# An attention and gated-MLP kernel: the first chunk of rows passes its first two projection blocks in two column halves, with another order of work around them

## The chip, the core and the metric

One core of one Trainium2 chip runs the kernel. Its engines take their instructions each in its own program order: TensorE (PE; its weight loads are listed apart as PEld), VectorE (DVE), ScalarE (ACT), GpSimd (POOL) and SyncE (SP), which here only starts transfers. The metric is the device time of one execution in microseconds (us), lower is better.

## The reference, cut to what matters

```python
x = A_x                                     # (1, 2048, 576), float32
xn = _layernorm(x, axis=-1)                 # (x - mean) / sqrt(var + 1e-5), per row
s = _A_ref(xn, A_wqkv, A_wo)                # attention: 32 heads of 18, then @ wo
g = _silu(_B_ref(xn, B_w_gate, B_w_up, B_w_down))   # ((xn Wg) * (xn Wu)) Wd, F = 4608
return x + s * g

def _A_ref(x, wqkv, wo):
    qkv = (x @ wqkv) ...                    # 576 -> 3 * 576
    p = softmax(q k^T * 18 ** -0.5)
    return (p v) ... @ wo
```

## The kernel before

The 2048 rows are worked in four chunks of 512, each of four tiles of 128 rows. The change lies wholly in the first tens of microseconds, in which chunk 0 is normalised, turned and multiplied with the first q and k weights. The rest of the program (attention, the gated MLP and the output projection, some 2500 us) stands in the same order before and after.

A product is made nearly float32-exact out of two float32r parts: a "high" copy, rounded on ScalarE, and a "low" rest, subtracted on another engine. So a column tile `xc` of a chunk has nine slices (four of 128 features high, the same four low, and slice 8, which holds the last 64 features high in its lower and low in its upper partitions), and one block of 128 output features is 14 matmuls, listed in `PAIRS`: nine with high weights, then five with low ones. There are nine blocks (0 to 8) for q and k.

The steps for chunk 0, with the lines of the profile:

- `load_x` (L289) loads the four row tiles into `xin`; `w_fetch` (L105, L109) loads weights into `wraw`, whose two buffers hold two blocks each, and `w_last` loads the last 64 features of a second block into `wl`. All go through SP's queue, in program order.
- `norm` takes statistics on VectorE (L298, L299) and a square root on ScalarE (L300). `norm_apply` then takes the reciprocal and the offset on VectorE (L308, L310), scales the tile on ScalarE (L311) and copies the last 64 columns beside themselves on GpSimd (L312). Chunks 2 and 3 scale on VectorE instead (L314, L316).
- `w_now` splits the weights of a buffer (`w_piece`): high on ScalarE (L451; for blocks 0 and 1 on VectorE, L449), low on GpSimd (L452).
- `to_columns` turns the tiles on TensorE (20 transposes of 128x128; L345 for chunk 0, L354 otherwise) into five PSUM banks of 512 columns, and converts each bank: high on ScalarE (L357, L361), low on VectorE (L358, L362).
- `qk_block(b, c)` multiplies block b with chunk c (L368, 14 matmuls of 512 columns) into a PSUM bank (`pa` or `pb`, two buffers each, in turn), and ends it: high on ScalarE (L371), low on VectorE (L372), both into `hl`, which SP stores to `sqk` (L378).

The program calls, for chunk 0: loads; `norm(0)`; `w_now(0)` (blocks 0, 1); `to_columns(0)`; `w_now(1)` (blocks 2, 3); `norm(1)`; the fetch of blocks 4 and 5; then blocks 0, 1, 2; `to_columns(1)`; `w_now(2)` (blocks 4, 5); blocks 3, 4, 5, with `norm(2)` and the split of the v weights (`v_split`, L414, L415) among them.

## Time and profile before

| | |
|---|---|
| median of 3 runs | 2564.52 us (2563.38 to 2564.65) |
| the profiled execution | 2566.68 us; its span from first to last instruction is 2564.9 us |
| TensorE busy | 2544.2 us, 99% of the span |
| VectorE, ScalarE, GpSimd busy | 1933.2, 1473.1, 618.9 us (75%, 57%, 24%) |
| mean granted TensorE clock | 0.999 |

The profiled execution took 2.16 us more than the median of the others. A row of a timeline gives the start, the duration (of all its instructions together, if it is several), the engine, the line, the operation with output and input, the count, and in brackets how long the engine had been idle and what ended that. Starts within one engine may lie closer than durations, since instructions overlap at their ends.

### The profile page before, as it was taken

How to read it: one execution, taken by the hardware profiler on the slowest of the kernel's cores; microseconds unless marked ns; L12 is line 12 of the kernel's file. 1: busy time of each engine (PE TensorE's matmuls, PEld its weight loads, DVE VectorE, ACT ScalarE, POOL GpSimd, SP SyncE). 2: the span in 40 equal slices, each digit the busy share in tenths (PEclk: the TensorE clock that was granted, in tenths of full speed). 3: DMA queues.
4: the chain of work that ended last, by engine and by line, in shares of the span. 5: the costliest groups of instructions: out<-in, count | busy, mean ns of one | idle time of the engine just before them, and what ended most of it. 6: DMA issues, size and time to landing. Idle time of an engine off the chain costs nothing.

```text
span 2564.9 us, 59227 instructions
## 1 busy us (share of the span) xinstructions
PE 2544.2 (99%) x24360; PEld 2115.4 (82%) x24360; DVE 1933.2 (75%) x3377; ACT 1473.1 (57%) x2712; POOL 618.9 (24%) x687
## 2 busy tenths in 40 slices
PE   8999999999999999999999999999999999999998
PEld 7899888787888888878888888778888888888878
DVE  6208678877778888777878888777889887778537
ACT  5222666666666655556666665555656656556651
POOL 3214334443421111112311111111111121111125
PEclk9999999999999999999999999999999999999999
DMA  7796889889775656576766566565666666664567
GB/s 246 234 293 163 222 220 244 222 217 248 199 222 173 183 174 185 173 183 186 214 201 174 172 178 184 168 178 154 180 204 164 175 190 176 178 175 142 160 194 248
DMA packets 203979, 499.87 MB, mean 195 GB/s; under 512 B 57744, under 2 KB 125200, under 8 KB 165948
## 3 DMA queue, kind: packets, MB, share of 16 engines
q1 hardware_dynamic: 193020, 482.86, 66.7%
q0 software_dynamic: 9952, 11.74, 1.7%
q8 instruction: 192, 3.15, 0.5%
q10 hardware_dynamic: 736, 1.47, 0.2%
q14 instruction: 79, 0.65, 0.1%
HBM read 307.49 MB, written 107.61 MB: 162 GB/s over the span
## 4 chain that ended last, share of the span: by engine, by line
PE 95%; DMA 2%; DVE 2%; ACT 0%; SPq 0%; POOL 0%; issue 0%; ACTq 0%; DVEq 0%
PE pg L703 35%; PE pg L667 17%; PE pg L749 15%; PE pa L624 11%; PE pb L656 9%; PE pg L423 2%; PE pa L368 2%; PE pb L368 2%; PE pg L1295 1%; DVE mx L626 0%; DMA sqk<-hl 0%; PE pa L1295 0%; PE pb L1295 0%; DMA hx<-hs 0%; DMA xi<-in_A_x_dram 0%; DMA gin<-sg 0%
## 5 line engine op out<-in xcount | busy, mean ns | idle before, releaser
L626 DVE TENSOR_REDUCE mx<-pa 128x1 f32<-128x512 f32 x2048 | 1364.7, 686 | 222.7 <-PE pa L624 114.1
L658 ACT ACTIVATE pt<-pb 128x512 f32<-128x512 f32 x2048 | 1160.8, 598 | 532.9 <-PE pb L656 477.2
L703 PE MATMUL pg<-xc,wgu 64*128 64x512 f32 x7722 | 1358.1, 388 | 0.0
L703 PEld LDWEIGHTS pg<-xc,wgu 64*128 64x128 f32 x7722 | 1048.2, 184 | 36.0 <-DVE acc L775 0.2
L656 PE MATMUL pb<-pair,ring 64*128 64x512 f32 x2016 | 784.6, 395 | 2.6 <-DMA pair<-mt 2.6
L624 PE MATMUL pa<-pair,ring 64*128 64x512 f32 x2008 | 778.2, 393 | 1.1 <-DVE mx L626 1.1
L749 PE MATMUL pg<-wd,hs 64*128 64x288 f32 x3408 | 582.2, 292 | 0.3 <-DVE acc L777 0.2
L749 PE MATMUL pg<-wd,hx 64*128 64x288 f32 x3360 | 567.7, 292 | 0.0
L749 PEld LDWEIGHTS pg<-wd,hs 64*128 64x128 f32 x3408 | 489.0, 185 | 5.5 <-issue 0.8
L720 POOL TENSOR_TENSOR hs<-us,hs 128x512 fp32r<-128x512 f32 x144 | 186.3, 1293 | 1262.6 <-ACT hs L719 1251.5
L749 PEld LDWEIGHTS pg<-wd,hx 64*128 64x128 f32 x3360 | 477.9, 185 | 3.0
L667 PE MATMUL pg<-pt,vt 128*32 128x512 f32 x4096 | 454.8, 594 | 1.0 <-DVE acc L777 0.9
L624 PEld LDWEIGHTS pa<-pair,ring 64*128 64x128 f32 x2008 | 364.9, 184 | 68.3 <-issue 51.1
L656 PEld LDWEIGHTS pb<-pair,ring 64*128 64x128 f32 x2016 | 366.0, 184 | 9.5 <-issue 2.9
L667 PEld LDWEIGHTS pg<-pt,vt 128*32 128x32 f32 x4096 | 125.5, 110 | 284.7 <-issue 278.3
L777 DVE TENSOR_TENSOR acc<-acc,pg 128x288 f32<-128x288 f32 x544 | 231.6, 443 | 26.4 <-PE pg L749 22.7
L673 DVE TENSOR_TENSOR oc<-oc,pg 128x512 f32<-128x512 f32 x69 | 47.2, 685 | 217.3 <-PE pg L667 217.2
L719 ACT ACTIVATE hs<-us 128x512 fp32r<-128x512 f32 x144 | 91.0, 632 | 140.2 <-DVE us L715 139.2
L206 POOL TENSOR_TENSOR wgu<-wraw,wgu 128x384 fp32r<-128x384 f32 x129 | 129.5, 1020 | 98.3 <-ACT wgu L205 81.5
L671 ACT ACTIVATE oc<-pg 128x512 f32<-128x512 f32 x32 | 19.1, 598 | 188.3 <-PE pg L667 181.8
L646 POOL DMA_DIRECT2D pair<-mt x128 | 77.9, 614 | 178.5 <-DVE mt L641 171.9
L715 DVE TENSOR_TENSOR us<-pg,us 128x512 f32<-128x512 f32 x144 | 98.5, 684 | 26.3 <-PE pg L703 18.0
(147 smaller groups left out, 1394.4 us busy)
## 6 DMA issues: line engine op xcount, KB each, us to landing
wgu<-swg SPq DMA_DIRECT2D x94, 1152.0 KB
hx<-hs SPq DMA_DIRECT2D x138, 512.0 KB
wd<-swd SPq DMA_DIRECT2D x50, 1152.0 KB
swg<-wgu SPq DMA_DIRECT2D x36, 1152.0 KB
pair<-sqk SPq DMA_DIRECT2D x192, 144.0 KB
ring<-sqk SPq DMA_DIRECT2D x384, 72.0 KB
swd<-wd SPq DMA_DIRECT2D x18, 1152.0 KB
sqk<-hl SPq DMA_DIRECT2D x32, 512.0 KB
```

The source lines that it names most:

```text
L206: nc.gpsimd.tensor_tensor(w[:, 9 + b:12 + b, :], raw[:, b:b + 3, :], w[:, b:b + 3, :].bitcast(FT), op=OP.subtract)
L368: nc.tensor.matmul(p, wq[b, a], xcs[c][:, e, :], start=n == 0, stop=n == len(PAIRS) - 1)
L624: nc.tensor.matmul(p, q[rows, t * 128:(t + 1) * 128], k[rows, c * 512:(c + 1) * 512], start=True, stop=True)
L626: nc.vector.tensor_reduce(mx[h][:, t, c:c + 1], p, axis=AX.X, op=OP.max)
L656: nc.tensor.matmul(p, k[rows, t * 128:(t + 1) * 128], q[rows, c * 512:(c + 1) * 512], start=True, stop=True)
L658: nc.scalar.activation(pt[t, c], p, AF.Exp, scale=scale)
L667: nc.tensor.matmul(p[32 * c:32 * c + 32, :], vt[h // 2][:, t, 6 * (h % 2):6 * (h % 2) + 32], pt[t, c], start=t == ts[0], stop=t == ts[-1])
L703: nc.tensor.matmul(ps, gw[n][half[r], a, :], xg[i][half[r], e, :], start=k == 0, stop=k == len(TERMS) - 1)
L715: nc.vector.tensor_tensor(h32, ps, h32, op=OP.mult)
L720: nc.gpsimd.tensor_tensor(hj[:, 1, :], h32, hj[:, 0, :].bitcast(FT), op=OP.subtract)
L749: nc.tensor.matmul(ps[:, 0:HALF], (hx if k else hs)[u][half[r], j, a, s * 128:(s + 1) * 128], dw[u][half[r], k, j, e, :], start=n == 0, st ...
L777: nc.vector.tensor_tensor(a, a, ps[:, 0:HALF], op=OP.add)
```

## The change

The new function `first_products` does what `norm(0)`, `w_now(0)`, `to_columns(0)`, `w_now(1)`, `norm(1)` and blocks 0 and 1 of chunk 0 did. Row tiles 0 and 1 (columns 0 to 255) are turned, converted and multiplied as one half, tiles 2 and 3 as another: conversions and matmuls have 256 columns instead of 512. Ahead of them TensorE does 26 transposes of the identity into an idle bank. Tile 0 is scaled on ScalarE, tiles 1 to 3 on VectorE. The high weights of blocks 0 and 1 are made on ScalarE. In three of the four halves the matmuls with low weights of the first eight slices stand earlier (`soon`). `w_now(1)` and the first two statistics of chunk 1 stand ahead of the end of block 0. On SP the loads of tiles 2 and 3 stand behind the first weights, those of chunk 1 behind the weights of blocks 2 and 3, and the fetch of blocks 4 and 5 behind the stores of blocks 0 and 1. `to_columns(1)` follows block 3 instead of block 2.

```diff
@@ load_x, to_columns, qk_block @@
-        xin[c] = ep.tile([128, 4, D], FT, name="xin", bufs=2)
-        for t in range(4):
+        if c not in xin:
+            xin[c] = ep.tile([128, 4, D], FT, name="xin", bufs=2)
+        for t in ts:
...
+        qk_product(b, c, p, slice(0, 512))
+        qk_end(b, c, p)
+
+    def qk_product(b, c, p, cols):
...
@@ -445,10 +444,7 @@
     def w_piece(i, at, n, b, k0, src):
 
         w, low = w_tile(i)
-        if i == 0 and b < 2:
-            nc.vector.tensor_copy(w[:, at:at + n, :], src)
-        else:
-            nc.scalar.activation(w[:, at:at + n, :], src, AF.Copy)
+        nc.scalar.activation(w[:, at:at + n, :], src, AF.Copy)
         nc.gpsimd.tensor_tensor(w[:, low + at:low + at + n, :], src, w[:, at:at + n, :].bitcast(FT), op=OP.subtract)
         for k in range(k0, k0 + n):
             wq[b, k if k < 4 else 8] = w[:, at + k - k0, :]
@@ -482,6 +478,99 @@
                 for part in range(2):
                     nc.sync.dma_start(sx[c, 8, :, part, :], src[64 * part:64 * part + 64])
 
+    def first_products():
+
+        xn = xns[0] = ep.tile([128, 4, 640], FT, name="xn", bufs=1)
+        xc = xcs[0] = c_tile(0)
+        ps = [bank("g", 3) if k < 4 else bank("a", 2) for k in range(5)]
+        out = [bank("b", 2), bank("a", 2)]
+        nqk[0] += 2
+        idle = bank("b", 2)
+        for n in range(26):
+            nc.tensor.transpose(idle[:, 0:128], ident, ident)
+
+        def scales(t):
+            mv, rs = stat[0, t]
+            nc.vector.reciprocal(rs[:, 1:2], rs[:, 0:1])
+            if t == 0:
+                nc.vector.scalar_tensor_tensor(rs[:, 2:3], mv[:, 0:1], -1.0, rs[:, 1:2], op0=OP.mult, op1=OP.mult)
+
+        def apply(t):
+            mv, rs = stat.pop((0, t))
+            if t == 0:
+                nc.scalar.activation(xn[:, t, 0:D], xin[0][:, t, :], AF.Identity, scale=rs[:, 1:2], bias=rs[:, 2:3])
+            else:
+                nc.vector.tensor_scalar(xn[:, t, 0:D], xin[0][:, t, :], mv[:, 0:1], rs[:, 1:2],
+                                        op0=OP.subtract, op1=OP.mult)
+            nc.gpsimd.tensor_copy(xn[:, t, D:640], xn[:, t, 512:D])
+
+        def turn(ts, ks):
+            for t in ts:
+                for k in ks:
+                    nc.tensor.transpose(ps[k][:, t * 128:(t + 1) * 128], xn[:, t, k * 128:(k + 1) * 128], ident)
+
+        def part(b, g, pairs):
+            cols = slice(256 * g, 256 * g + 256)
+            for a, e in pairs:
+                nc.tensor.matmul(out[b][:, cols], wq[b, a], xc[:, e, cols], start=(a, e) == PAIRS[0],
+                                 stop=(a, e) == PAIRS[-1])
+
+        def high(g, k):
+            cols = slice(256 * g, 256 * g + 256)
+            nc.scalar.activation(xc[:, k if k < 4 else 8, cols], ps[k][:, cols], AF.Copy)
+
+        def low(g, k):
+            cols = slice(256 * g, 256 * g + 256)
+            rows, d, e = (slice(0, 128), k, 4 + k) if k < 4 else (slice(64, 128), 8, 8)
+            nc.vector.tensor_tensor(xc[rows, e, cols], ps[k][rows, cols], xc[rows, d, cols].bitcast(FT), op=OP.subtract)
+
+        for t in (0, 1):
+            norm_stats(0, t)
+        for t in (0, 1):
+            scales(t)
+            apply(t)
+        w_piece(0, 0, 5, 0, 0, raws[0][:, 0:5, :])
+        turn((0, 1), range(4))
+        turn((0, 1), (4,))
+        high(0, 0)
+        high(0, 1)
+        norm_stats(0, 2)
+        for k in range(2, 5):
+            high(0, k)
+        low(0, 0)
+        low(0, 1)
+        scales(2)
+        for k in range(2, 5):
+            low(0, k)
+        apply(2)
+        w_piece(0, 5, 4, 1, 0, raws[0][:, 5:9, :])
+        last1()
+        norm_stats(0, 3)
+        scales(3)
+        apply(3)
+        first, second = PAIRS[:9], PAIRS[9:]
+        soon = first[:4] + second[:4] + first[4:] + second[4:]
+        part(0, 0, soon)
+        part(1, 0, first)
+        turn((2,), range(5))
+        part(1, 0, second)
+        turn((3,), range(5))
+        for k in range(5):
+            high(1, k)
+            low(1, k)
+        w_now(1)
+        last3()
+        for t in (0, 1):
+            norm_stats(1, t)
+        for b in range(2):
+            part(b, 1, soon)
+            qk_end(b, 0, out[b])
+            norm_apply(1, b)
+            norm_stats(1, b + 2)
+        norm_apply(1, 2)
+        norm_apply(1, 3)
+        xns.pop(0)
+
     def x_first(n):
 
         (i, k), (slot, part) = divmod(n, 9), divmod(n, 2)
@@ -497,39 +586,37 @@
             nc.sync.dma_start(xg[i][64 * r:64 * r + 64, k, :].bitcast(FT), xcs[0][r0:r0 + 64, j, :].bitcast(FT))
 
     raws = {}
-    load_x(0)
-    w_fetch(0)
+    load_x(0, (0, 1))
+    raws[0] = wpool.tile([128, 9, 128], FT, name="wraw", bufs=2)
+    w_load(raws[0][:, 0:5, :], 0, 0, 5)
+    load_x(0, (2, 3))
+    w_load(raws[0][:, 5:9, :], 1, 0, 4)
     last1 = w_last(2, 9, 1)
-    load_x(1)
     w_fetch(1)
     last3 = w_last(2, 10, 3)
-    norm(0)
-    w_now(0)
-    last1()
-    to_columns(0)
-    w_now(1)
-    norm(1)
-    last3()
+    load_x(1)
+    first_products()
     w_fetch(2)
     last5 = w_last(2, 11, 5)
     v_fetch(0)
     for c in range(NCH):
         if c + 2 < NCH:
             load_x(c + 2)
-        for b in range(3):
+        first = 3 if c else 4
+        for b in range(0 if c else 2, first):
             qk_block(b, c)
         if c + 1 < NCH:
             to_columns(c + 1)
         if c == 0:
             w_now(2)
             last5()
-        for b in range(3, 6):
+        for b in range(first, 6):
             qk_block(b, c)
-            if b < 5 and c + 2 < NCH:
-                norm(c + 2, (0, 1) if b == 3 else (2, 3))
+            if b < first + 2 and c + 2 < NCH:
+                norm(c + 2, (0, 1) if b == first else (2, 3))
             if c in (1, 2):
                 x_store(c, range(3 * (b - 3), 3 * (b - 2)))
-            if (c, b) in ((0, 3), (1, 3)):
+            if (c, b) in ((0, 4), (1, 3)):
                 v_split(c)
             if (c, b) == (0, 5):
                 v_fetch(1)
```

On TensorE (PE) at the start, before: the transposes of the fourth tile (those of the other three stand ahead, alike), then blocks 0 and 1; `xn` is the normalised tile, `xcx` the column tile, `wgu` and `wq` hold weights of blocks 0 to 5:

```order
L345 MATMUL pg<-ident,xn 128x128 x4
L345 MATMUL pa<-ident,xn 128x128
L368 MATMUL pb<-xcx,wgu 128x512 x14
L368 MATMUL pa<-xcx,wgu 128x512 x8
L368 MATMUL pa<-xcx,wq_174 128x512
L368 MATMUL pa<-xcx,wgu 128x512 x4
L368 MATMUL pa<-xcx,wq_174 128x512
```

And now:

```order
L490 MATMUL pb<-ident 128x128 x26
L510 MATMUL pg<-ident,xn 128x128 x8
L510 MATMUL pa<-ident,xn 128x128 x2
L515 MATMUL pb<-xcx,wgu 128x256 x14
L515 MATMUL pa<-xcx,wgu 128x256 x8
L515 MATMUL pa<-xcx,wq_216 128x256
L510 MATMUL pg<-ident,xn 128x128 x4
L510 MATMUL pa<-ident,xn 128x128
L515 MATMUL pa<-xcx,wgu 128x256 x4
L515 MATMUL pa<-xcx,wq_216 128x256
L510 MATMUL pg<-ident,xn 128x128 x4
L510 MATMUL pa<-ident,xn 128x128
```

Ten transposes stand ahead of the first products instead of 20, and the other ten between those of block 1.

On ScalarE (ACT) of the changed kernel, from the last conversion of chunk 0 to the end of block 1 (`rs` is a square root of a statistic, `hl` the end of a block):

```order
L520 ACTIVATE xcx<-pa 128x256
L447 ACTIVATE wgu<-wraw 128x640
L447 ACTIVATE wgu<-wraw 128x512
L447 ACTIVATE wq_216<-wl 128x128
L301 ACTIVATE rs<-mv,eps 128x1 x2
L370 ACTIVATE hl<-pb 128x512
L312 ACTIVATE xn<-xin,rs 128x576
L301 ACTIVATE rs<-mv,eps 128x1
L370 ACTIVATE hl<-pa 128x512
```

The weights of blocks 2 and 3 and two square roots of chunk 1 stand ahead of block 0's end; before, all four square roots and all four scalings of chunk 1 did.

On ScalarE a little further on, before: the ends of three blocks, then the conversions of chunk 1 and the weights of blocks 4 and 5:

```order
L371 ACTIVATE hl<-pb 128x512
L371 ACTIVATE hl<-pa 128x512
L371 ACTIVATE hl<-pb 128x512
L357 ACTIVATE xcx<-pg 128x512 x3
L357 ACTIVATE xcx<-pa 128x512
L361 ACTIVATE xcx<-pb 128x512
L451 ACTIVATE wq_174<-wraw 128x640
L451 ACTIVATE wq_174<-wraw 128x512
L451 ACTIVATE wq_174<-wl 128x128
L371 ACTIVATE hl<-pa 128x512
```

And now:

```order
L370 ACTIVATE hl<-pb 128x512
L370 ACTIVATE hl<-pa 128x512
L350 ACTIVATE xcx<-pg 128x512 x3
L350 ACTIVATE xcx<-pb 128x512
L354 ACTIVATE xcx<-pa 128x512
L447 ACTIVATE wq_216<-wraw 128x640
L447 ACTIVATE wq_216<-wraw 128x512
L447 ACTIVATE wq_216<-wl 128x128
L370 ACTIVATE hl<-pb 128x512
```

The rows on ScalarE are the same, but on TensorE the block that follows the transposes of chunk 1 was block 3, whose weights are made long before, and is now block 4, whose weights are these.

## Rows read from the trace of the kernel before

**Rows 1.** The page's first part: busy time, share of the span, instructions.

```profile
PE 2544.2 (99%) x24360; PEld 2115.4 (82%) x24360; DVE 1933.2 (75%) x3377; ACT 1473.1 (57%) x2712; POOL 618.9 (24%) x687
```

**Rows 2.** Waits of TensorE from 19.6 to 131 us: total, times, longest.

```profile
PE pg L423 <- POOL wv L415: 0.4, 1, 0.4
```

**Rows 3.** Timeline of TensorE's matmuls, first 72 us.

```profile
6.84 1.12 PE L345 MATMUL pg<-ident,xn 128*128 128x128 f32 x4 [6.84 <-ACT xn L311]
...
11.82 3.02 PE L368 MATMUL pb<-xcx,wgu 128*128 128x512 f32 x8
...
16.56 1.98 PE L368 MATMUL pa<-xcx,wgu 128*128 128x512 f32 x8
...
19.73 3.34 PE L368 MATMUL pb<-xcx,wgu 128*128 128x512 f32 x14
...
22.91 1.47 PE L354 MATMUL pg<-ident,xn 128*128 128x128 f32 x12
...
24.66 0.60 PE L354 MATMUL pb<-ident,xn 128*128 128x128 f32 x4
...
28.30 3.33 PE L368 MATMUL pb<-xcx,wq 128*128 128x512 f32 x14
...
60.08 11.54 PE L423 MATMUL pg<-wv,xcx 128*128 128x288 f32 x85 [0.35 <-POOL wv L415]
```

**Rows 4.** Timeline of DMA starts on SP, first 17 us.

```profile
0.75 1.81 SPq L289 DMA_DIRECT2D xin<-in_A_x_dram  x4
...
3.08 1.18 SPq L109 DMA_DIRECT2D wraw<-in_A_wqkv_dram  x2
...
10.35 0.59 SPq L105 DMA_DIRECT2D wraw<-in_A_wqkv_dram  x1
```

**Rows 5.** Timeline of VectorE, first 32 us.

```profile
5.40 0.21 DVE L299 BATCH_NORM_AGGREGATE mv<-st 128x2 f32<-128x12 f32 x1
...
6.14 0.82 DVE L298 BATCH_NORM_STATS2 st<-xin 128x6 f32<-128x288 f32 x2 [0.31 <-DMA xin<-in_A_x_dram]
...
11.80 2.48 DVE L358 TENSOR_TENSOR xcx<-pg,xcx 128x512 fp32r<-128x512 f32 x4 [1.90 <-ACT xcx L357]
...
17.10 1.02 DVE L310 SCALAR_TENSOR_TENSOR rs<-mv,rs 128x1 f32<-128x1 f32 x1
...
31.85 0.58 DVE L314 TENSOR_SCALAR xn<-xin,mv,rs 128x576 f32<-128x576 f32 x1
```

**Rows 6.** Timeline of ScalarE, first 28 us.

```profile
4.72 0.29 ACT L300 ACTIVATE rs<-mv,eps 128x1 f32<-128x1 f32 x1 [2.70 <-DVE mv L299]
...
11.17 2.07 ACT L357 ACTIVATE xcx<-pg 128x512 fp32r<-128x512 f32 x4 [0.68 <-PE pg L345]
...
14.47 1.26 ACT L451 ACTIVATE wgu<-wraw 128x640 fp32r<-128x640 f32 x2 [0.74 <-DMA wraw<-in_A_wqkv_dram]
...
25.72 0.64 ACT L361 ACTIVATE xcx<-pb 128x512 fp32r<-128x512 f32 x1
26.20 1.31 ACT L451 ACTIVATE wq<-wraw 128x640 fp32r<-128x640 f32 x2
```

**Rows 7.** The page's costliest groups, 288 columns on VectorE: busy us, mean ns of one, idle.

```profile
L777 DVE TENSOR_TENSOR acc<-acc,pg 128x288 f32<-128x288 f32 x544 | 231.6, 443 | 26.4 <-PE pg L749 22.7
```

**Rows 8.** Groups by form, 288 columns on ScalarE, first 140 us: columns alike.

```profile
L429 ACT ACTIVATE vo<-pg 128x288 f32<-128x288 f32 x12 | 4.7, 412 | 15.4 <-PE pg L423 8.8 <-DMA sv<-vo 6.4
```

**Rows 9.** Timeline of GpSimd, first 22 us.

```profile
15.29 2.82 POOL L452 TENSOR_TENSOR wgu<-wraw,wgu 128x640 fp32r<-128x640 f32 x2 [1.51 <-ACT wgu L451]
```

**Rows 10.** Timeline of TensorE's weight loads around the first products.

```profile
10.51 0.87 PEld L345 LDWEIGHTS pg<-ident,xn 128*128 128x128 f32 x4
...
12.31 0.29 PEld L368 LDWEIGHTS pb<-xcx,wgu 128*128 128x128 f32 x1 [0.20 <-ACT xcx L357]
12.80 0.19 PEld L368 LDWEIGHTS pb<-xcx,wgu 128*128 128x128 f32 x1 [0.20 <-ACT xcx L357]
```

**Rows 11.** Busy time by stretch; the last three are granted clock, DMA share, GB/s.

```profile
6.80:11.80 5.00, 4.75 (x20) 3.86 (x20) 2.81 (x13) 3.78 (x8) 2.31 (x5) 1.00 0.98 304
```

More of the change, by code (lines that the diff above doesn't have):

```diff
@@ L284, with load_x @@
     xin, xns = {}, {}
-    def load_x(c):
-        xin[c] = ep.tile([128, 4, D], FT, name="xin", bufs=2)
-        for t in range(4):
+    def load_x(c, ts=range(4)):
+        if c not in xin:
+            xin[c] = ep.tile([128, 4, D], FT, name="xin", bufs=2)
+        for t in ts:
             nc.sync.dma_start(xin[c][:, t, :], x2[c * 512 + t * 128:c * 512 + t * 128 + 128, :])
@@ L329, with c_tile @@
     nqk = [0]
+    def c_tile(c):
+        if c < 2:
+            return pp.tile([128, 9, 512], FR, name="xcx", bufs=2)
+        return xcp.tile([128, 9, 512], FR, name="xc")
     def to_columns(c):
         xn = xns.pop(c)
-        if c < 2:
-            xc = pp.tile([128, 9, 512], FR, name="xcx", bufs=2)
-        else:
-            xc = xcp.tile([128, 9, 512], FR, name="xc")
-        xcs[c] = xc
-        ps = {}
-        if c == 0:
-            for k in range(5):
-                ps[k] = bank("g", 3) if k < 4 else bank("a", 2)
-            for t in range(4):
-                for k in range(5):
-                    nc.tensor.transpose(ps[k][:, t * 128:(t + 1) * 128], xn[:, t, k * 128:(k + 1) * 128], ident)
-        for k in range(5):
-            if c:
-                if k in (3, 4):
-                    ps[k] = bank("a" if nqk[0] % 2 else "b", 2)
-                    nqk[0] += 1
-                else:
-                    ps[k] = bank("g", 3)
-                for t in range(4):
-                    nc.tensor.transpose(ps[k][:, t * 128:(t + 1) * 128], xn[:, t, k * 128:(k + 1) * 128], ident)
-            p = ps[k]
+        xc = xcs[c] = c_tile(c)
+        for k in range(5):
+            if k in (3, 4):
+                p = bank("a" if nqk[0] % 2 else "b", 2)
+                nqk[0] += 1
+            else:
+                p = bank("g", 3)
+            for t in range(4):
+                nc.tensor.transpose(p[:, t * 128:(t + 1) * 128], xn[:, t, k * 128:(k + 1) * 128], ident)
             if k < 4:
@@ L366, in qk_block, with qk_end @@
         nqk[0] += 1
+        qk_product(b, c, p, slice(0, 512))
+        qk_end(b, c, p)
+    def qk_product(b, c, p, cols):
         for n, (a, e) in enumerate(PAIRS):
-            nc.tensor.matmul(p, wq[b, a], xcs[c][:, e, :], start=n == 0,
+            nc.tensor.matmul(p[:, cols], wq[b, a], xcs[c][:, e, cols], start=n == 0,
                              stop=n == len(PAIRS) - 1)
+    def qk_end(b, c, p):
         hl = pp.tile([128, 2, 512], FR, name="hl", bufs=3)
@@ L483, in x_store @@
                     nc.sync.dma_start(sx[c, 8, :, part, :], src[64 * part:64 * part + 64])
+    def first_products():
[16 more added lines that the diff above has]
+                nc.scalar.activation(xn[:, t, 0:D], xin[0][:, t, :], AF.Identity, scale=rs[:, 1:2], bias=rs[:, 2:3])
+            else:
+                nc.vector.tensor_scalar(xn[:, t, 0:D], xin[0][:, t, :], mv[:, 0:1], rs[:, 1:2],
[48 more added lines that the diff above has]
+        turn((3,), range(5))
+        for k in range(5):
+            high(1, k)
[12 more added lines that the diff above has]
+        xns.pop(0)
```

1 line of the change is left out of this document (removed).

## The prediction

> **What bounds the kernel now.** I read first the page's busy times: TensorE is busy 99% of the span, the others 75% and less [rows 1]. So a change is worth what it does to TensorE's idle or slow time. The waits of TensorE are next: after 19.6 us and up to 131 us there is one, of 0.4 us, for GpSimd [rows 2], on the low part of the v weights, at 60.08 [rows 3]. What the change can gain thus lies before 19.73 us, where block 2 begins. TensorE's timeline of that stretch shows where it goes. Nothing runs until the first tile is scaled at 6.84. The 20 transposes then last until the first product at 11.82. Block 0 takes 16.56 - 11.82 = 4.74 us, while block 1 takes 19.73 - 16.56 = 3.17 us [rows 3], which is 0.227 us for each of 14 matmuls, the dense pace: block 0 waited for its conversions.
>
> **A bound for the gain.** At the dense pace, that of chunk 1, a transpose takes (24.66 - 22.91)/16 = 0.109 us [rows 3]. 20 of them and two blocks are 20 x 0.109 + 2 x 3.17 = 8.52 us. The first transposes need tile 0, which still goes the same way (load, statistics, ScalarE), so they stay at 6.84. Before, that work took 19.73 - 6.84 = 12.89 us; no more than 12.89 - 8.52 = 4.4 us can be saved ahead of block 2. With the 0.35 us of the later wait that is under 5.1 us, the 0.2% of the time below which I take a measurement to show no change.
>
> **The first half.** The 26 dummy transposes run while TensorE had nothing to do and end before 6.84: even at the slow pace, (0.87 - 0.23)/3 = 0.21 us between weight loads with the last load at the tile's mean of 0.22 [rows 10], they take 5.5 us from about 1.4 us, when the identity is made. Tile 1 is scaled on VectorE (0.58 us [rows 5]) beside tile 0 on ScalarE, so its transposes follow at once. These ten end at about 6.84 + 1.09 = 7.9 instead of the 11.8 of all twenty.
>
> **The chain that ends last** from here on is VectorE's, since it now has statistics, subtractions and scalings in one row. Its prices: two statistics 0.82, with their aggregate 0.86 + 0.21 = 1.07 us [rows 5]; scaling 0.58; a square root on ScalarE 0.29 [rows 6] with a hop of about 0.04 on each side, 0.37. The 256-column work is not in the trace. A subtraction takes 0.443 us for 288 columns [rows 7], and four of 512 take 2.48 [rows 5]; the mean of one there, about 0.68, puts starts at (2.48 - 0.68)/3 = 0.60. By the line through both widths I take 0.41 long and 0.33 apart. Bounds are nothing saved below 288 columns (0.443) and half of 0.60. ScalarE likewise: 0.412 for 288 [rows 8], 2.07 for four of 512 [rows 6], so 0.385 long and 0.27 apart. A 256-column matmul lies between a transpose (0.109) and a 288-column one (11.54/85 = 0.136 [rows 3]); I take 0.122. Four halves are then 56 x 0.122 = 6.8 us, against 6.34 for two blocks; this cost of 0.5 us is hidden, because conversions set the pace.
>
> When does tile 2 land? Before, the third tile was issued some 1.66 us after the start (four issues in 1.81 from 0.75 [rows 4]), and VectorE waited for it until 6.14 [rows 5]: 4.5 us. Weights issued at 10.35 [rows 4] ended a wait at 14.47 [rows 6]: 4.1 us. Now two tiles (0.9), a weight piece (about 0.45, as a tile) and two small ones (1.18 [rows 4]) stand ahead, so tile 2 is issued at about 3.3 and lands at 7.4 to 7.8. It can't be used before VectorE is done with tile 1, about 6.75. I take 7.4.
>
> From there in VectorE's order: statistics of tile 2 until its next instruction 0.99; two subtractions 0.66; reciprocal 0.13; three subtractions 0.99; scaling 0.59; statistics of tile 3 with the aggregate 1.07; square root 0.37; reciprocal 0.13; scaling 0.59. Sum 5.5, so tile 3 is scaled at 12.9. One transpose and its delay 0.3, a conversion 0.4, five subtractions 1.65: chunk 0 is converted at 15.3. Then the statistics of two tiles of chunk 1 stand ahead of block 0's end: 2 x 0.98 + 0.1 = 2.05, square root 0.37, high part 0.60, low part 0.69. The end is done at 19.0. Its bank is the one that block 2 needs (two buffers in turn, block 0, the idle bank, block 2), so block 2 waits for it, although TensorE is through with block 1 by about 17.3.
>
> VectorE also gets slower beside GpSimd: an offset that should take some 0.2 us took 1.02 at 17.10, and ended at 18.12 with GpSimd's two subtractions (15.29 + 2.82 = 18.11) [rows 5, 9]. The scaling of tile 3 falls beside such work. I add 0.1, with a bound of 0.5. **Block 2 begins at 19.1** (18.3 with tile 2 at 6.75, 19.9 with 7.8 and 0.5 more), against 19.73.
>
> **The second wait.** Two blocks (6.34) and the 20 transposes of chunk 1 (2.18) end at 19.1 + 8.52 = 27.6. Now follows block 4. Its high weights stand on ScalarE behind block 3's end and five conversions of chunk 1. Block 3 ends at 25.45; with 0.16 of delay and 0.49 for its end ScalarE begins the conversions at 26.1. They start 0.48 apart (25.72 to 26.20 [rows 6]), so the weights start at 28.5, and the first 640 columns, 0.77 of the 1.31 for both pieces [rows 6], are there at 29.3. Before, block 3 stood in this place and hid all of it, and block 4 began at 28.30 [rows 3]. So at equal work done the changed kernel is at **29.3 - 28.30 = 1.0 us late**: 0.6 us won at block 2, 1.7 us lost in a new wait. Block 4's low weights on GpSimd (1.57 of the 2.82 for two [rows 9]) are ready at 30.9, just ahead of its tenth matmul (29.3 + 9 x 0.227 = 31.3).
>
> **Queues.** On SP the fetch of blocks 4 and 5 is now behind the stores of blocks 0 and 1, and those wait for block 1's end, about 21.9 (behind a scaling, a statistic and a square root). The fetch of block 4's pieces is issued from 23 to 24.2; 4.1 us after the start of the last one, 28.1, they are there, 0.4 us before ScalarE asks. Each later microsecond costs one. Block 5's, the v weights and chunk 2 are asked for later still. A later start of everything may be partly taken back at 60.08: there TensorE waited 0.35 us for GpSimd, whose part depends on transfers rather than on TensorE. I count half.
>
> **Sum.** 1.0 - 0.2 = +0.8 us: 2566.68 + 0.8 = 2567.5 for the profiled execution. That one lay 2.16 us above the median, so the median becomes **2565.3**. The bounds of tile 2 and of GpSimd's share make it -0.2 to +1.8.
>
> **The rivals.**
>
> *The dummies do not raise the clock.* Before, the transposes from 6.84 to 11.8 went at the lower of the two levels (1.2 GHz), at about 0.21 us instead of 0.109, although the column of the granted clock says 1.00 and TensorE was busy 4.75 of 5.00 us [rows 11]. A weight load at 12.31 took 0.29 us, the one at 12.80 took 0.19 [rows 10]: the clock rose within 1 us of the first product, after 5 us of transposes. That speaks for transposes that count, but does not settle it. If they don't, the ten transposes take 1.0 us longer; the first conversions come that much later, of which VectorE, busy with statistics until about 8.4, feels 0.6 to 0.9. The time: 2566.1. The Trainium skill, "TensorE: Matmul & The Clock Gate", section "Part 4: PE-mode transpose", states that the full clock does not engage for transposes, which do not count as busy in the same way; by that rule this rival holds. The trace has the low pace all through the transposes, as the rule would have it, and the rise too soon after the first product to lie in products alone.
>
> *Neither queue's order costs.* If statistics, square roots and conversions turn out quick enough for block 2 to follow block 1 at 17.3 and block 4 the transposes, block 4 begins at 17.3 + 8.52 = 25.8, 2.5 us early: 2562.0. For it: the orders are only some tenths apart in places. Against: both waits come from fixed sequences whose parts are rows.
>
> *Late weights* (the other side). If the stores and loads on SP's queue delay the fetch of block 4, TensorE stands for it in full. From 28.5 on each microsecond adds one; slower by 5.1 us needs a landing at about 33, 9 us after the issue, twice what the rows show. At 33 it gives 2570.
>
> **How the numbers follow.** My forecast 0.63, no cost of the orders 0.17, dummies without effect 0.15, late weights beyond 1 us 0.05, of which 0.03 beyond 5.1. The range takes in the forecast with its bounds, the clock rival and the greater part of the way to the second: 2562.8 to 2567.4. Faster by over 0.2% is all but excluded by the bound of 4.4 us: 0.02. Slower 0.04, within 0.2% 0.94.
>
> **What would show it.** Right: the first real transposes at about 6.84, the dummies over before; TensorE idle ahead of block 2 for its bank, released by VectorE's end of block 0, at about 19; and idle again ahead of block 4 at about 27.6, released by ScalarE's weights. Wrong: transposes of tile 0 0.2 us apart (clock); no idle time at these two places (a gain of over 2 us); block 4 released by a transfer; or any new wait of TensorE after 35 us, where I expect none.

## The result and the profile after

The changed kernel takes **2567.5 us** (median of 21 runs, 2564.7 to 2570.9) beside 2564.2 us of the kernel before on the same chip (21 runs, 2562.2 to 2566.3). The ratio is 1.0014, with a 95% interval of 1.0008 to 1.0019: slower by 2.1 to 4.9 us, 3.3 in the middle. That is less than the 0.2% below which the prediction takes a measurement to show no change, and in the direction that it forecast; but it forecast +0.8 us, and the range ended at 2567.4, 0.1 us short. The profiled execution took 2567.11 us with a span of 2565.3.

TensorE's timeline of the changed kernel, matmuls only; the bracket gives the idle time before a group and what ended it:

```profile
1.44 5.02 PE L490 MATMUL pb<-ident 128*128 128x128 f32 x26 [1.44 <-DVE ident L279]
6.85 1.09 PE L510 MATMUL pg<-ident,xn 128*128 128x128 f32 x8 [0.39 <-ACT xn L501]
...
8.09 0.66 PE L515 MATMUL pb<-xcx,wgu 128*128 128x256 f32 x2
9.70 1.85 PE L515 MATMUL pb<-xcx,wgu 128*128 128x256 f32 x12 [0.94 <-ACT xcx L520]
...
18.33 0.40 PE L515 MATMUL pa<-xcx,wq 128*128 128x256 f32 x2
20.17 3.47 PE L365 MATMUL pb<-xcx,wgu 128*128 128x512 f32 x14 [1.44 <-DVE hl L371]
...
30.62 1.66 PE L365 MATMUL pb<-xcx,wq 128*128 128x512 f32 x6 [1.62 <-ACT wq L447]
...
58.38 15.02 PE L422 MATMUL pg<-wv,xcx 128*128 128x288 f32 x112
73.24 2.93 PE L365 MATMUL pb<-xc,wgu 128*128 128x512 f32 x12
```

Read it beside [rows 3]. The real transposes begin at 6.85 as before, but run through in 1.09 us for eight; the first product comes at 8.09 instead of 11.82. Block 1 is through by 18.7, one microsecond ahead of before. There the lead ends: block 2 waits 1.44 us for VectorE's end of block 0 and starts at 20.17 (19.73 before), and block 4 waits 1.62 us for its weights on ScalarE and starts at 30.62 (28.30 before, in the same place of the work). The 112 products of the v blocks no longer show the 0.35 us wait of 60.08, so part is given back here; the second pair of chunks begins at 73.24. In the trace of before the same group begins at 71.46: **1.8 us late**.

```profile
71.46 3.36 PE L368 MATMUL pb<-xc,wgu 128*128 128x512 f32 x14
```

What led to block 2, on VectorE:

```profile
6.18 0.58 DVE L503 TENSOR_SCALAR xn<-xin,mv,rs 128x576 f32<-128x576 f32 x1
7.98 0.82 DVE L299 BATCH_NORM_STATS2 st<-xin 128x6 f32<-128x288 f32 x2 [1.22 <-DMA xin<-in_A_x_dram]
...
13.04 0.74 DVE L503 TENSOR_SCALAR xn<-xin,mv,rs 128x576 f32<-128x576 f32 x1
14.62 1.42 DVE L525 TENSOR_TENSOR xcx<-pg,xcx 128x256 fp32r<-128x256 f32 x4 [0.83 <-ACT xcx L520]
16.07 0.43 DVE L525 TENSOR_TENSOR xcx<-pa,xcx 64x256 fp32r<-64x256 f32 x1
16.53 0.82 DVE L299 BATCH_NORM_STATS2 st<-xin 128x6 f32<-128x288 f32 x2
...
17.51 0.77 DVE L299 BATCH_NORM_STATS2 st<-xin 128x6 f32<-128x288 f32 x2
...
19.42 0.69 DVE L371 TENSOR_TENSOR hl<-pb,hl 128x512 fp32r<-128x512 f32 x1 [0.90 <-ACT hl L370]
```

VectorE stands 1.22 us for tile 2, which lands at 7.98; tile 3 is scaled at 13.78, and chunk 0 is converted at 16.5; two statistics of chunk 1 follow, and only then, with the high part on ScalarE between, the low part of block 0's end. It is over at 20.11, and block 2 starts 0.06 us later.

And what led to block 4, on ScalarE, where before the last conversions were followed by the weights at 26.20, with a whole block of products still to cover them [rows 6]:

```profile
26.90 0.60 ACT L370 ACTIVATE hl<-pa 128x512 fp32r<-128x512 f32 x1 [0.32 <-ACT hl L370]
27.39 1.57 ACT L350 ACTIVATE xcx<-pg 128x512 fp32r<-128x512 f32 x3
28.82 0.63 ACT L350 ACTIVATE xcx<-pb 128x512 fp32r<-128x512 f32 x1
29.30 0.65 ACT L354 ACTIVATE xcx<-pa 128x512 fp32r<-128x512 f32 x1
29.83 0.74 ACT L447 ACTIVATE wq<-wraw 128x640 fp32r<-128x640 f32 x1
30.74 0.63 ACT L447 ACTIVATE wq<-wraw 128x512 fp32r<-128x512 f32 x1 [0.17 <-DMA wraw<-in_A_wqkv_dram]
```

Five conversions of chunk 1 stand ahead of the weights, which start at 29.83; their first piece is rounded at 30.57, and TensorE goes on. The first piece had landed in time; the second, for block 5, came 0.17 us late, from SP's queue, where the fetch stands behind three stores that wait for the block ends:

```profile
10.28 2.01 SPq L290 DMA_DIRECT2D xin<-in_A_x_dram  x4
20.14 4.16 SPq L377 DMA_DIRECT2D sqk<-hl  x3
24.39 0.61 SPq L105 DMA_DIRECT2D wraw<-in_A_wqkv_dram  x1
25.06 1.82 SPq L109 DMA_DIRECT2D wraw<-in_A_wqkv_dram  x2
```

### The profile page after: what moved, and what is told of

It reads as the page before. It is cut to its first block, busy times and chain, and to the rows that moved or that the text cites. A ratio compares the mean times of both kernels' runs of the same rounds, so it can differ in the third digit from the quotient of the medians.

```text
span 2565.3 us, 59339 instructions
## 1 busy us (share of the span) xinstructions
PE 2545.6 (99%) x24414; PEld 2115.5 (82%) x24414; DVE 1934.3 (75%) x3380; ACT 1471.1 (57%) x2716; POOL 616.5 (24%) x687
## 4 chain that ended last, share of the span: by engine, by line
PE 97%; DVE 1%; DMA 0%; issue 0%; ACT 0%; POOL 0%; SPq 0%; ACTq 0%; DVEq 0%
PE pg L790 35%; PE pg L754 18%; PE pg L836 16%; PE pa L711 11%; PE pb L743 9%; PE pg L422 2%; PE pb L365 2%; PE pa L365 2%; PE pg L1382 1%; PE pa L1382 1%; PE pb L1382 1%; DVE mx L713 0%; DMA pair<-mt 0%; DVE acc L864 0%; DVE us L802 0%; DMA wraw<-in_A_wqkv_dram 0%
## 5 line engine op out<-in xcount | busy, mean ns | idle before, releaser
L758 ACT ACTIVATE oc<-pg 128x512 f32<-128x512 f32 x32 | 19.1, 598 | 188.3 <-PE pg L754 181.8
```

## The experiments

The theory: the loss is made by the two new waits, each from a fixed order on one engine. Rivals: the dummies, the queue of transfers, or something later in the kernel. "Second pair" below is the start of the first product of the second pair of chunks in the profile: 71.46 before, 73.24 after. Kernels sent together share the runs of before; with 11 runs of each kernel the interval of a ratio is some 2.3 us to either side, so positions in the traces carry the argument and the medians only accompany it.

**Each kernel again** (no edit).

> The kernel before once more, unchanged, for a second profile: by the runs so far the changed kernels are about 1.6 us slower than the difference of the starts in the profiles says. Theory (the first profile of before is a slow one at its start, where TensorE's clock rose only at 12.3 to 12.8 us): block 2 begins at 18.3 to 19.5 instead of 19.73, or the pause around 255 us costs less than the 1.6 us of the first profile. Rival (the start of before is the same in each execution): 19.73 within 0.1, and the same pause.

> The changed kernel once more, unchanged, beside the next two on the same chip: 2567.5 again. Of the 3.3 us that it lost, its first profile shows 1.8 ahead of the second chunk's blocks. Theory (in some executions TensorE's clock falls to the lower level in one of the two new waits, as it did for 1.7 us of loss in the profile of the kernel that normalises first): if this profile is such an execution, block 4 takes about 5 us instead of 3.3. Rival (the rest lies behind 70 us): block 4 takes 3.3 to 3.5 us.

Before: block 2 at 19.65, block 4 at 28.21, second pair at 70.69, and the same loss at 255 us (1.7 us, below); the rival held. After: block 2 at 19.34 behind a wait of 1.43, block 4 at 29.79 behind 1.61, second pair at 72.41, 1.7 us later; median 2568.5 beside 2564.1, ratio 1.0016 (1.0007 to 1.0025). Block 4 takes 3.47 us, so the clock fell in neither wait of this execution: here too the rival held. So both waits are in every trace of the changed kernel, 0.8 us of either start is scatter, and the difference of the two is not.

The scatter has a place. The rows of this profile, then those of a third one of the changed kernel (the one with only the pause at 255 us filled, below):

```profile
7.16 0.82 DVE L299 BATCH_NORM_STATS2 st<-xin 128x6 f32<-128x288 f32 x2 [0.40 <-DMA xin<-in_A_x_dram]
19.34 3.47 PE L365 MATMUL pb<-xcx,wgu 128*128 128x512 f32 x14 [1.43 <-DVE hl L371]
29.79 3.47 PE L365 MATMUL pb<-xcx,wq 128*128 128x512 f32 x14 [1.61 <-ACT wq L447]
```

```profile
7.29 0.82 DVE L299 BATCH_NORM_STATS2 st<-xin 128x6 f32<-128x288 f32 x2 [0.45 <-DMA xin<-in_A_x_dram]
19.48 3.49 PE L365 MATMUL pb<-xcx,wgu 128*128 128x512 f32 x14 [1.44 <-DVE hl L371]
29.95 3.48 PE L365 MATMUL pb<-xcx,wq 128*128 128x512 f32 x14 [1.62 <-ACT wq L447]
```

Tile 2 lands at 7.16, 7.29 and, in the first profile, 7.98. Block 2 begins 12.2 us behind the landing in all three, and block 4 10.5 us behind block 2: what scatters is the transfer, and the row of work behind it doesn't.

**The bank of block 2** (first wait removed): the idle bank is taken first, so that block 2 gets it and not block 0's.

```
+        idle = bank("b", 2)
         out = [bank("b", 2), bank("a", 2)]
         nqk[0] += 2
-        idle = bank("b", 2)
```

> Only the first of the two new waits is taken away: the dummy transposes and block 0 change PSUM banks, so that block 2's bank is the idle one and not block 0's. Theory (two new waits and nothing else): block 2 begins at 18.6 instead of 20.17; then the fourth tile of chunk 1, scaled at about 26.1 in either kernel, holds the transposes up, and the weights of block 4 are ready at about 30.1; block 4 begins at 30.1 instead of 30.62, so 0.5 us are gained on the changed kernel, to about 2567.0. Rival (each wait costs its length, independently): 1.5 us gained, 2566.0. Rival (the loss is not in these waits): no gain, 2567.5.

Block 2 starts at 17.88 without a wait, but block 4 at 30.03 behind a wait of 2.48 us for the same weights; second pair 73.75, median 2567.6 beside 2564.1. ScalarE reaches the weights earlier, at the end of conversions that began at 26.28, and now waits 0.43 us for their transfer. The whole gain at the first wait goes into the second.

**The weights of block 4** (second wait removed): fetched ahead of the block ends, and rounded ahead of chunk 1's conversions.

```
+        w_fetch(2)
+        last5 = w_last(2, 11, 5)
+        v_fetch(0)
         w_now(1)
         last3()
...
-    first_products()
-    w_fetch(2)
-    last5 = w_last(2, 11, 5)
-    v_fetch(0)
+    last5 = first_products()
...
-        if c + 1 < NCH:
-            to_columns(c + 1)
         if c == 0:
             w_now(2)
             last5()
+        if c + 1 < NCH:
+            to_columns(c + 1)
```

> Only the second new wait is taken away: the weights of blocks 4 and 5 are fetched ahead of the stores of blocks 0 and 1, and split on ScalarE ahead of the conversions of chunk 1. Theory (two new waits): block 4 follows the transposes at 28.85 instead of 30.62, 1.8 us gained; at 0.5 us over the kernel before at this place, and with the v weights' wait of 0.35 us also gone, the time is that of the kernel before within 0.5 us, 2564.2 to 2565. Rival (what is lost lies behind the prologue or in the 256-column halves): 2567 or more.

ScalarE now has the weights first, and block 4 follows the transposes:

```profile
27.22 1.25 ACT L447 ACTIVATE wq<-wraw 128x640 fp32r<-128x640 f32 x2
...
28.56 1.57 ACT L350 ACTIVATE xcx<-pg 128x512 fp32r<-128x512 f32 x3
```

Block 4 at 28.58 with no wait, second pair 71.17, median 2565.6 beside 2564.1 (ratio 1.0006, 0.9997 to 1.0015). Tile 2 landed at 7.32 and 7.80 in these two profiles; with 12.2 + 10.45 us behind it the changed kernel would have begun block 4 at 29.97 and 30.45. So the first edit (30.03) gains nothing and the second (28.58) 1.9 us: this wait is where the loss was.

**Both edits.**

> Both waits are taken away. Theory: block 4 begins at about 28.3, as before (28.30), since the transposes of chunk 1 now wait for its fourth tile (scaled at about 26.1); 2563.8 to 2564.5. Rival (waits add up, nothing else comes late): 27.0, 2563. Rival (the loss is elsewhere): 2567 or more.

```profile
17.84 3.36 PE L365 MATMUL pb<-xcx,wgu 128*128 128x512 f32 x14
...
25.43 1.20 PE L348 MATMUL pg<-ident,xn 128*128 128x128 f32 x9 [0.43 <-ACT xn L312]
...
27.25 3.45 PE L365 MATMUL pb<-xcx,wq 128*128 128x512 f32 x14
```

Second pair 69.96, 1.5 and 0.7 us ahead of before's two profiles; median 2564.2 beside 2564.1. With the two waits gone the change costs nothing, and its halves bring the lead that they can, less 0.43 us for chunk 1's fourth tile.

**The dummies** taken out of the changed kernel, and put alone into the kernel before.

```
         idle = bank("b", 2)
-        for n in range(26):
-            nc.tensor.transpose(idle[:, 0:128], ident, ident)
```

> The changed kernel without its 26 dummy transposes. Theory (the clock's start hardly matters here, since VectorE waits until 7.98 for tile 2 and its statistics set the pace): the first ten transposes take 0.21 instead of 0.11 us each, block 2 begins 0 to 0.6 us later, 2567.5 to 2568.1. Rival (a low clock in the first half costs all along the chain): 1 to 2 us more, 2568.5 to 2569.5.

> The kernel before with the 26 dummy transposes alone. Theory (they raise the clock before the first real transposes, which in before go at the low pace): the fourth tile's transposes end 0.5 us earlier and block 0 runs at full pace; 0.5 to 1.0 us faster than before, 2563.0 to 2563.6. Rival (conversions set the pace, the clock doesn't matter): the time of before.

Without them, TensorE's timeline begins

```profile
6.83 1.97 PE L508 MATMUL pg<-ident,xn 128*128 128x128 f32 x8 [6.83 <-ACT xn L499]
8.60 0.64 PE L508 MATMUL pa<-ident,xn 128*128 128x128 f32 x2
8.88 2.55 PE L513 MATMUL pb<-xcx,wgu 128*128 128x256 f32 x14
```

Ten transposes last until 8.88 instead of 8.09: the low pace. Here VectorE is through with tile 2's statistics and waits 0.80 us for the first conversion; block 2 comes at 19.84, ahead of the changed kernel's first profile, in which tile 2 was late, but 0.4 to 0.5 us behind its other two. Second pair 73.82, median 2570.4 beside 2564.1 (1.0021, 1.0013 to 1.0030), beyond both forecasts. The trace explains 0.6 us of the 2.9 between the two medians (0.8 by the mean of the three profiles, 73.05). In the kernel before they change nothing: products from 11.80, block 2 at 19.71, second pair 71.44, median 2566.2 beside 2564.2 (1.0007, 0.9998 to 1.0016).

**Scaling of chunk 1 in one go**, on top of both edits: all of its tiles are scaled ahead of the two block ends. Then the same **with tile 2 loaded ahead of the first weights**.

```
-        for t in (0, 1):
-            norm_stats(1, t)
         for b in range(2):
             part(b, 1, soon)
+        norm(1)
+        for b in range(2):
             qk_end(b, 0, out[b])
-            norm_apply(1, b)
-            norm_stats(1, b + 2)
-        norm_apply(1, 2)
-        norm_apply(1, 3)
```

```
-    load_x(0, (0, 1))
+    load_x(0, (0, 1, 2))
...
-    load_x(0, (2, 3))
+    load_x(0, (3,))
```

> Both waits taken away, and chunk 1 is normalised in one go ahead of the ends of blocks 0 and 1. Theory: the fourth tile of chunk 1 is scaled at about 22 instead of 25.4, the transposes of chunk 1 don't wait, block 4 begins at 26.4 instead of 27.25; 2563.4. Rival (the ends of blocks 0 and 1 come late and hold up banks or stores): 2564.2 or more.

> As the one before, and row tile 2 is loaded ahead of the first weights. Theory (the chain that ends last starts with tile 2, which landed at 7.98 in the changed kernel and at 6.14 before): its statistics run from about 6.8, all that follows is 0.6 to 1.1 us earlier; 2562.4 to 2562.8. Rival (the first weights, now later, hold up ScalarE by as much): 2563.4 or more.

Both miss. The late ends hold up ScalarE, and block 4 waits for weights again, 1.85 us and 1.86 us. ScalarE itself stood for a store, 3.04 us in the first kernel and in the second

```profile
27.19 0.60 ACT L370 ACTIVATE hl<-pa 128x512 fp32r<-128x512 f32 x1 [3.05 <-DMA sqk<-hl]
```

since the ends have three buffers and the first store had begun late. The medians are 2567.5 and 2567.4 beside 2564.2. The first kernel shows something new, behind the wait of 1.85 us. TensorE's timeline, and its windows (busy time of PE, PEld, DVE, ACT, POOL; then granted clock, DMA share, GB/s):

```profile
29.44 5.06 PE L365 MATMUL pb<-xcx,wq 128*128 128x512 f32 x14 [1.85 <-ACT wq L447]
```

```profile
28.00:30.00 2.00, 0.56 (x2) 0.49 (x3) 0.69 (x1) 1.83 (x4) 0.53 (x1) 1.00 1.01 202
30.00:32.00 2.00, 2.00 (x8) 1.63 (x7) 1.38 (x3) 2.00 (x6) 2.00 (x2) 0.73 0.98 229
32.00:34.00 2.00, 2.00 (x6) 1.54 (x6) 1.80 (x3) 0.54 (x2) 2.00 (x5) 0.50 0.93 342
34.00:36.00 2.00, 2.00 (x10) 1.60 (x9) 0.83 (x2) 0.60 (x1) 0.33 (x1) 0.92 1.05 406
```

The granted clock is 0.50 for some 3.4 us (1.2 GHz instead of 2.4), and block 4 takes 5.06 us instead of 3.45: 2 x (0.27 + 0.50 + 0.08) = 1.7 us lost by the windows, on top of the wait. Behind the 1.86 us of the second kernel, and behind the 2.48 us of the first edit above, it doesn't fall.

**The waits filled, not shortened**: 12 and 14 transposes of the identity run into a free bank while TensorE waits for block 0's end and for block 4's weights; once in the changed kernel, once in the one without dummies.

```
+    def fill(n):
+        free = bank("g", 3, 0)
+        for _ in range(n):
+            nc.tensor.transpose(free[:, 0:128], ident, ident)
...
+        if c == 0:
+            fill(12)
         for b in range(0 if c else 2, first):
...
+        if c == 0:
+            fill(14)
         for b in range(first, 6):
```

> The changed kernel with both new waits kept, but filled with transposes of the identity into a free bank, 12 ahead of block 2 (1.3 us) and 14 ahead of block 4 (1.5 us). No wait gets shorter; what changes is that TensorE is not idle in them. Theory (falls of the clock in these waits cost the missing 1 us on average): 2566.3 to 2566.8, fewer executions at a mean clock of 0.998. Rival (the waits cost their length and nothing more): 2567.5, the time of the changed kernel.

> As the one before, but without the 26 dummies at the start, which cost the changed kernel 2.9 us when they were left out, though its profile was only 0.6 us later at the second chunk. Theory (that loss came from falls of the clock in the waits, more often without the dummies): filled waits give 2566.8 to 2567.5. Rival (the start itself is that much slower): 2570.

Medians 2566.8 and 2567.9 beside 2564.1, with the changed kernel at 2568.5 on the same chip. Block 4 starts no earlier (29.88 and 30.47), so a gain of 1.7 us would have to come from the clock; the intervals (1.0001 to 1.0019 and 1.0005 to 1.0023) don't settle it.

**One end ahead of the scalings, one behind** (both edits, with tile 2 loaded first).

```
+        part(0, 1, soon)
+        qk_end(0, 0, out[0])
+        part(1, 1, soon)
+        for t in range(4):
+            norm_apply(1, t)
+            if t < 2:
+                norm_stats(1, t + 2)
+        qk_end(1, 0, out[1])
```

> Both waits taken away and row tile 2 loaded ahead of the first weights, as in an earlier kernel whose block 3 waited for a store of block 0 before its end could be written; now block 0's end stands ahead of the scalings of chunk 1 and block 1's end behind them. Theory: no wait of TensorE ahead of block 2, of the transposes of chunk 1 or of block 4, which begins at about 26.5; 2562 to 2563, faster than the kernel before. Rival (another late item takes their place, or what was lost lies behind the prologue): 2564 or more.

No wait is left from block 2 (17.91) over block 4 (26.38) to 58 us, but then the v weights on GpSimd are late:

```profile
58.81 0.40 PE L422 MATMUL pg<-wv,xcx 128*128 128x288 f32 x1 [0.36 <-POOL wv L414]
59.56 11.53 PE L422 MATMUL pg<-wv,xcx 128*128 128x288 f32 x85 [0.35 <-POOL wv L414]
```

Second pair 70.92, median 2565.4 beside 2564.1 (ratio 1.0002, 0.9993 to 1.0011): the lead of 1.9 us at block 4 over before's first profile is 0.5 us here, and there is none over its second (70.69). That GpSimd's v weights bound what any such order can gain is argued from these waits, not tested.

**The pause at 255 us.** In the profile of before the clock falls behind 2.6 us in which TensorE waits for a transfer (its row, then the windows):

```profile
257.81 0.46 PE L656 MATMUL pb<-pair,ring 64*128 64x512 f32 x1 [2.63 <-DMA pair<-mt]
```

```profile
256.00:258.00 2.00, 0.19 (x2) 0.22 (x4) 0.16 (x1) 1.26 (x1) 1.46 (x2) 1.00 0.10 23
258.00:260.00 2.00, 2.00 (x14) 1.57 (x14) 0.69 (x1) 1.66 (x3) 0.00 (x0) 0.65 1.14 255
260.00:262.00 2.00, 2.00 (x13) 1.55 (x10) 0.69 (x1) 0.00 (x0) 1.42 (x1) 0.50 1.16 239
```

which is 2 x 0.35 + 2 x 0.50 = 1.7 us lost. In the first profile of the changed kernel it does not fall there, in the second it does. Of all 14 profiles without a fill in this pause ten show the fall, behind pauses of 2.34 to 3.24 us, and four don't, behind 2.60 to 3.65 us. To take this out, 22 transposes fill that pause in the kernel before, in the changed one, in the version with one end ahead, in the version with both edits, and, with the two waits filled too, in the changed kernel.

```
+            if (h, i) == (0, 0):
+                for _ in range(22):
+                    nc.tensor.transpose(p[:, 0:128], ident, ident)
             nc.tensor.matmul(p, k[rows, t * 128:(t + 1) * 128], q[rows, c * 512:(c + 1) * 512],
```

> The kernel before, with 22 transposes of the identity into the bank of the first score block, ahead of its first product: they fill most of the pause of 2.6 us in which TensorE waits at about 255 us for the pair's second half, and the product that follows overwrites them. No data waits longer. Theory (the clock falls behind that pause in part of the executions, and costs about 1.6 us there; how often it does so differs between the kernels, which makes up the part of the change's loss that the two new waits leave open): the rows 255 to 265 us show a granted clock of 1.00 in the profile, and the median falls by 0.5 to 1.6 us, to 2562.5 to 2563.6. Rival (the fall is given back later, since what follows waits for something else): no change, 2564.1.

> The changed kernel with the same 22 transposes in the same pause. Theory: the clock stays at 1.00 there, and what is left between this kernel and the one before with the fill is what the two waits of the first 31 us cost, 1.7 to 1.8 us at the second pair of chunks, with up to 0.7 more for falls of the clock in these waits: 1.7 to 2.5 us apart. Median 2564.5 to 2566. Rival (the offset lies elsewhere): the two stay 3.3 us apart, whatever the fill brings to both.

> The variant with one block end ahead of the scalings, early weights, idle bank first and tile 2 ahead of the weights, with the 22 transposes in the pause. It had no new wait in the first 31 us, and began the second pair of chunks at 70.92 (0.2 to 0.5 us ahead of before). Theory: with the pause filled it is level with the kernel before with its fill or up to 0.7 us ahead of it, 2562 to 2563.6. Rival (an offset that belongs to all variants of the change): about 1.3 us behind that kernel, as without the fills.

> The changed kernel with all three pauses filled: 12 and 14 transposes in the two new waits, 22 in the pause at 255 us; every wait for data stays as long as it was. Theory: no clock falls in a pause any more, and what is left is the length of the two waits, 1.7 to 2.0 us at the second pair of chunks: 2565 to 2565.4 beside 2563.2 of the kernel before with its fill. Rival (falls in the two waits are not what the rest is): as the changed kernel with the one fill at 255 us, 2566.7.

> The variant with both waits removed (idle bank allocated first, block 4's weights fetched and rounded earlier), with the 22 transposes in the pause at 255 us. It began the second pair of chunks 0.7 us ahead of the kernel before. Theory: level with the kernel before with its fill or up to 1 us ahead, 2562.2 to 2563.4. Rival (an offset of the changed kernel apart from the two waits and the clock): about 1 us behind it, 2564.2.

The kernel before with its fill, the same stretch:

```profile
256.00:258.00 2.00, 1.90 (x18) 1.64 (x18) 0.00 (x0) 1.05 (x1) 1.23 (x1) 1.00 0.21 63
258.00:260.00 2.00, 2.00 (x20) 1.67 (x18) 1.14 (x2) 1.66 (x3) 0.14 (x1) 1.00 1.27 272
260.00:262.00 2.00, 2.00 (x21) 2.00 (x20) 1.52 (x3) 0.00 (x0) 1.29 (x1) 1.00 1.02 215
```

In all five profiles the clock stays at 1.00 there. Medians: 2563.2 (before with the fill), 2566.7 (changed), 2563.0 (one end ahead), each beside 2564.1; then 2564.8 (changed, all three filled) and 2562.9 (both edits), beside 2564.9. The pause alone therefore does not close the gap: changed and before stay 3.5 us apart, as the rival had it. With the two waits filled as well, the changed kernel is level with the plain kernel before, and the two versions without the waits are 1.1 and 2.0 us under it. Their ratios, 0.9995 (0.9987 to 1.0004) and 0.9993 (0.9985 to 1.0002), do not exclude no change; no version is shown to beat the kernel before.

**Nine profiled executions side by side.** "Fall" is the time lost to the lower clock at 255 to 266 us, worked out from windows as above; the last column is time less fall less second pair.

| kernel | time, us | fall | second pair | rest |
|---|---|---|---|---|
| before | 2566.68 | 1.7 | 71.46 | 2493.5 |
| before, again | 2565.80 | 1.7 | 70.69 | 2493.4 |
| before, pause filled | 2565.45 | 0 | 71.14 | 2494.3 |
| changed | 2567.11 | 0 | 73.24 | 2493.9 |
| changed, again | 2568.19 | 1.7 | 72.41 | 2494.1 |
| changed, pause filled | 2566.68 | 0 | 73.51 | 2493.2 |
| changed, all filled | 2564.71 | 0 | 72.79 | 2491.9 |
| both edits | 2563.77 | 1.7 | 69.96 | 2492.1 |
| both edits, pause filled | 2564.04 | 0 | 70.47 | 2493.6 |

The rest is 2493.3 us, within 1.5, for all of them; the ten other profiles have 2491.5 to 2494.5. Its mean is 2493.7 for the three profiles of before and for the first three of the changed kernel, so in the profiles nothing behind the second pair belongs to the change: it is late there by 73.05 - 71.10 = 1.95 us (means of three and three), and the end inherits that.

## Why the prediction came out as it did

**Right.** The real transposes start at 6.85 (6.84 forecast); no more than the first 19 us could gain; block 2 waits for the bank that VectorE's end of block 0 frees, with the statistics ahead of it; block 4 waits for its weights behind five conversions on ScalarE; the fetch stands behind the stores on SP's queue and is in time for block 4 (its second piece, block 5's, is 0.17 us late in the first profile and 0.91 in the third, and TensorE waits for it in neither); no new wait follows. Each wait was confirmed by the edit that removes it, and the larger effect of the second, named as the place of the loss, by the first two experiments.

**The term that was mis-sized** is the start of block 2, "19.1", and with it that of block 4, "29.3": the row of VectorE's work behind tile 2 is longer than I reckoned. The first profile alone would blame the transfer, since tile 2 landed at 7.98 where I took 7.4. But it landed at 7.16 and 7.29 in the other two; 7.4 is close to the mean, 7.48. From the landing to block 2 it took 12.2 us in all three, and the sum has 11.7. In the first profile the ten subtractions of 256 columns, reckoned at 0.33 us apart (3.30 us), took 0.62 + 1.25 + 1.88 = 3.75 us. The first conversion was ready 0.84 us behind the scaling of tile 3, not 0.7. That scaling took 0.74 us instead of 0.58 while GpSimd's subtraction ran beside it (13.01 to 13.47), so the 0.1 added for GpSimd was needed. Small savings elsewhere gave 0.2 back.

From block 2 to block 4 it took 10.45 us in all three, not 10.2: ScalarE's first conversion of chunk 1 begins at 27.39, 0.88 behind the end of block 3 (20.17 + 6.34), where 0.65 stood in the sum. Block 4 thus began at 30.62, 29.79 and 29.95. The kernel before was at the same place at 28.30, 28.21 and 27.90 (the last with the pause filled). By the means, 30.12 and 28.14, the changed kernel is 2.0 us late in place of 1.0. At the v weights I counted 0.2 us back; that wait of 0.35 us is in two of the three profiles of before and in one of the three after, so it comes and goes in either kernel, and by the means nothing came back: 1.95 us at the second pair, where the sum had 0.8.

One reading of a row was wrong without effect. The wait that ended at 14.47 was for block 2's weights, the last of whose issues began at about 9.7 and not at 10.35; from there it took 4.8 us, not 4.1.

**The step from the profile to the median** failed too. The sum takes 2.16 us off because the profiled execution of before lay that far above its median, as if that of the changed kernel would. But 1.7 us of it were the fall at 255 us, which that execution had and the first profile of the changed kernel has not; its 2567.11 lies 0.4 us below its own median. That it comes close to the 2567.5 forecast for the profiled execution is luck: the second pair was 1.0 us later than the sum has it, and a fall of 1.7 us was missing.

**What the median has beyond that**: 3.3 against 1.95, which lies just under the interval's lower end, 2.1. A term that the sum lacks is the clock: a wait of 1.85 us was shown to be followed by 3.4 us at 1.2 GHz in one kernel, at a cost of 1.7 us, and filling both waits of the changed kernel without shortening them went with a median 1.7 us lower on the same chip (and 1.9 lower, on another chip, with the pause at 255 us filled too). Its own three profiles show no such fall in the first 40 us. The mean granted clock of each execution, also of those without a profile, is on record to three places; one step is 2.6 us, so only means of many say something. It is 0.9991 over 141 executions of before and 0.9988 over 32 of the changed kernel, some 2.2 and 3.0 us lost. Filling the two waits took it from 0.9985 to 0.9992 (11 executions each, same chip), 1.6 us, as much as the median moved. So by this estimate some 0.8 us of the rest is a lower clock, and the filled waits point to where. That the falls stand behind these two waits no profile of the changed kernel shows; what is then left, about half a microsecond, and the larger loss without dummies (2570.4) stay open.

**The rivals.** *The dummies do not raise the clock* fell: the 26 take 5.02 us, and the eight transposes behind them stand 0.116 us apart (6.85 to 7.78), close to the dense pace of 0.109; without them ten last from 6.83 to 8.88. The tile of the identity shows the rise inside the dummies, where TensorE had done nothing else; the columns are least, middle and greatest ns, and first and last start:

```profile
L490 PEld LDWEIGHTS pb<-ident x26: 139/230/230, 1.4 to 6.1; 128*128 128x128 f32 x26
```

Weight loads of 230 ns at first, of 139 at the end: both levels in one run of transposes. The Trainium skill, "TensorE: Matmul & The Clock Gate", section "Part 4: PE-mode transpose", has it that transposes don't count towards the full clock; here they alone brought it, and the trace disagrees. *Neither queue's order costs* fell with the two waits; and its price of 2.5 us was too high, since with both waits removed the kernel is level with before (2564.2 beside 2564.1). *Late weights* fell as a rival in size, though the transfer is close behind: 0.17 and 0.91 us late for the second piece in two profiles, and 0.43 us for the first once ScalarE asks earlier.

## What to carry to other kernels

When one engine takes over work of another, follow its whole row to the next thing that TensorE needs from it (here the freeing of a bank), and then ask which row sets the block after that: removing the first of two waits in series gained nothing, because the second stood within a microsecond behind it. A transfer's landing scattered by 0.8 us between executions of one kernel, and every later step inherits that: take a second profile, and measure the work from the landing, before a late start is explained by either. A wait of two microseconds on TensorE can cost almost two more by the clock behind it, in some executions and not in others, so look at the granted clock behind each pause before two profiles are compared, and before the distance of one profile from its median is carried over to another kernel.

## What the runs showed of the hardware

A pause of 1.85 us (28 to 30 us) or 2.6 us (255 us) may be followed by about 3.4 us at a granted clock of 0.50, a loss of 1.7 us; of the profiles of one and the same kernel one shows it and another doesn't. The length of the pause alone doesn't decide: at 255 us the clock fell behind pauses of 2.34 to 3.24 us in ten profiles and not behind 2.60 to 3.65 us in four, and it did not fall behind waits of 1.86 and 2.48 us ahead of block 4. 22 identity transposes in the pause kept the clock at 1.00 in all five kernels that had them. At the start the column of the granted clock reads 1.00 while the weight loads take 230 ns (the row of the 26 above; the column reads 1.00 from 1 to 7 us), so there the pace of the instructions has to be read, not the column. And the store of a block's result, issued late, held ScalarE for 3.05 us through the three buffers of its source, a wait that no compute row announces.
